# Agent attention and top-1 experts on one core: transfers queued in the order asked for, and longer distances between a chunk's steps

## The chip, the cores and the metric

The kernel runs on one core of a Trainium2 chip. The core has five engines with an instruction stream each: TensorE (PE in the profile; its weight loads are listed as PEld), VectorE (DVE), ScalarE (ACT), GpSimd (POOL) and SyncE (SP), which does nothing here but start transfers and read a few registers. Transfers run on 16 DMA engines. An engine works through its own stream in order and waits at an instruction until what that needs is there. The metric is the device time of one execution in microseconds; the kernel before was timed three times.

## The reference

For each of four batches: agent attention over N = 11456 tokens of 128 numbers with 49 agents, then a mixture of eight experts in which each token goes to one expert.

```python
def sm(a, b):
    s = scale * (a @ b.transpose(0, 2, 1))
    e = np.exp(s - s.max(-1, keepdims=True))
    return e / (e.sum(-1, keepdims=True) + 1e-09)
a2k = sm(agents, k)
agent_v = a2k @ v
x = (sm(q, agents) @ agent_v).reshape(-1, D)
expert_idx = np.argmax(x @ w_gate, axis=1)
...
    xe = x[mask]
    h = np.maximum(xe @ w1[e], 0.0)
    out[mask] = gate_w[mask, None] * (h @ w2[e])
```

All tensors are float32. There are 45824 tokens in all; F, the hidden size of an expert, is 1024.

## The kernel before

**Tiling.** A batch is cut into 12 chunks of tokens: 11 of 1024 (128 partitions, 8 tokens in each) and a remainder of 192. Keys, queries and values of a chunk are loaded into a tile `ld` (512 KB, 11 buffers), squared and summed on ACT for a scale (`squares`, L348), split into two float16 halves `hl` (ACT makes the high half, DVE the low one, L392 and L394), and for keys and queries turned over by a DMA transpose into `hT` (`turn_over`, L415; two buffers for keys, two for queries). PE makes the scores of the chunk from `hT` (L461 to L463). Of queries, ACT takes the exponential E, which is stored to DRAM (`exps`, L699), split into float16 halves in one of two tiles `mm` (L705, L709) and turned over by another DMA transpose into `M` (`eturn`, L712).

**The experts' main loop.** Most tokens of a batch go to one expert, which is worked off for all tokens. `experts` (L1294 to L1346) makes 23 groups of up to 512 tokens times 8 slices of F: 184 steps a batch, 736 in all. One step is two matmuls of 512 columns on PE (L1299, L1300, which read `M`), the high and low float16 halves of their ReLU on ACT (L1305) and on DVE (L1306), and 12 matmuls of 128 columns (L1320), which belong to the step five before. Four PSUM tiles `ph` hold the results of the first two. After eight steps DVE multiplies the group by its gate (L1333) and SP stores it (L1339). Tokens of other experts are gathered in 14 blocks late in the last batch and after it.

**How the work is interleaved.** The attention of batch b + 1 runs beside the experts of batch b. The order is a table of times counted in steps: `at(t, f)` (L275) puts f on a heap, `after(dt, f)` (L279) puts it dt steps behind the event that is running, and the loop at L1396 takes the events in order of time. Step 0 of batch b has time 184 b. Keys of a batch start at `KS`, one chunk every `KT` = 9 steps, and their scores come `KL` steps behind the squares; queries start at `QA`, 8, then 13 steps apart, and their scores also come `KL` behind (`KLL` for the later chunks of the last batch). Values come 5.3 steps apart. `DTR` is the distance from the low half to the transpose into `hT`, `DTE` from the halves of E to the transpose into `M`, `DEX` from the exponential to the store of E, `DST` from the gate's product to the store of a group. A load is asked for when the squares of the second use before it are (`load`, L298: `AHEAD` = 3 uses with the present one).

The keys' exponentials are added up chunk by chunk on POOL into `es` (L555). Then `agentvalues(0)` reduces `es` to `e1` on DVE (L609), and `agentvalues(1)` sums `e1` over the partitions on PE (L614); both are due one and two steps behind the last chunk's exponentials (L891 to L893). POOL also ranks the tokens of the batch that is ending (`leftover_ranks`, L930, L935 to L952) in that time.

**What sets an engine's order.** The framework schedules each engine's stream from the traced program with a model of its own: an instruction that is ready by the model may be taken ahead of others traced earlier. `issue_after` (L1403) ties what an event issues on PE, ACT and DVE behind the step's instruction on the same engine that lies 1.5, 2 and 2.5 steps back. SP has no such tie before the change, apart from a gate at the start (L220): its stream is what the model made of it.

Of the kernel before, what the change touches and what calls it, by code (L numbers as in the profile page):

```python
# [45 lines left out]
KS0, KT0, KL0, VT0, VL0, QS0, QT0, QL0 = -200, 2, 4, 2, 1, -172, 3, 2.5  # L46
VE, T1, TF0, TF1, TL, TLM, Q0 = 12, 1.75, 3, 1.5, 18, 10, 2

KS, KT, VT, VL, VL4, TW0, TW1, DW = -208, 9, 5.3, 8, 5, 8, 2.5, 1
QA, QB, QC, QB3, KL, LL, UD, RG, D1, DL = -20, 8, 13, 10.5, 9, 9.5, 2, 0.7, 0.5, 0  # L50

KS1 = []

KLL, LLL = 11, 11
LX, LMG, LSP = 8, 4, 2.5

SLA, SLD, SLP = 2, 2, 1.5

DTR, DTE, DEX, DST, DXS = 2, 0.5, 2, 2, 0.5

LAG = 5

# [13 lines left out]
def agent_moe_kernel(ctx, tc, q, k, v, agents, wg, w1, w2, out):  # L76
    nc = tc.nc
# [11 lines left out]
    NCK = len(chunks)  # L89
# [177 lines left out]
    def pick(x, c):  # L267
        return x[c % len(x)]
# [4 lines left out]
    now, count = [0], [0]  # L273

    def at(t, f, *a):  # L275
        count[0] += 1
        heapq.heappush(events, (t, count[0], f, a))
# [10 lines left out]
    def attention(b):  # L288
        st = state[b]
        base = b * steps  # L290
        first, last = b == 0, b + 1 == B
# [573 lines left out]
        ks, kt, kl, vt, vl = (KS0, KT0, KL0, VT0, VL0) if first else (KS, KT, KL, VT, VL)  # L865
        dl = 0 if first else DL
# [12 lines left out]
        tv = tk + 4  # L879
# [8 lines left out]
            at(base + t + 2 * dl, kexp3, c)  # L888
            at(base + t + vl, values, c)
        ta = tv + vt * (NCK - 1) + vl + 2  # L890
        te = tv + vt * (NCK - 1) + 2 * dl + (T1 if first else 1)  # L891
        at(base + te, agentvalues, 0)
        at(base + te + (0.1 if first else 1), agentvalues, 1)  # L893
        at(base + ta, agentvalues, 2)
        at(base + ta + 1.5, agentvalues, 3)
        at(base + ta + 2.5, agentvalues, 4)
# [251 lines left out]
    def weights_ahead(u):  # L1148
        T, i, _ = where[u]
        ws[u] = block_weights(T, i, tiles(w1e=(ldp, "ld"), w2e=(ldp, "ld")))  # L1150

    def weights_split(u, j, eng):
        x, (T, i, _) = ws[u][j], where[u]
        m = T["m1" if j == 0 else "m2"][:, i:i + 1]
        tag = slots[(2 * u + j) % len(slots)]
        hl = wsp[u, j] = (ldp if tag == "ld" else xpool).tile(
            [P, 2, FF], F16, tag=tag, name="wsp", **({} if tag == "ld" else dict(bufs=HLB if tag == "hl" else HTB[tag[2:]])))
        nc.scalar.activation(hl[:, 0, :], x, AF.Copy, scale=m)
        if eng == "D":
            nc.vector.scalar_tensor_tensor(hl[:, 1, :], x, m, hl[:, 0, :], op0=ALU.mult, op1=ALU.subtract)  # L1160
        else:
            nc.scalar.activation(x, x, AF.Copy, scale=m)
            nc.gpsimd.tensor_tensor(hl[:, 1, :], x, hl[:, 0, :], op=ALU.subtract)

    def block_layer1(u, hf):

        xs, w = blocks[u][0], wsp[u, 0]
        wv = w.rearrange("d s (p t) -> d s t p", t=FT)
        ph = psH.tile([P, 512], F32, tag="h", name="ph")
        for i in range(4):  # L1170
            o, t = ph[:, i * P:(i + 1) * P], hf * 4 + i
            nc.tensor.matmul(o, wv[:, 0, t, :], xs[:, 0, :], start=True, stop=False)
            nc.tensor.matmul(o, wv[:, 0, t, :], xs[:, 1, :], start=False, stop=False)
            nc.tensor.matmul(o, wv[:, 1, t, :], xs[:, 0, :], start=False, stop=True)
        hh = hpool.tile([P, 2, 512], F16, tag="h", name="hh")
        nc.scalar.activation(hh[:, 0, :], ph, AF.Relu)
        nc.vector.scalar_tensor_tensor(hh[:, 1, :], ph, 0.0, hh[:, 0, :], op0=ALU.max, op1=ALU.subtract)
        bh[u, hf] = hh

    def block_layer2(u, hf):  # L1180

        wv = wsp[u, 1].rearrange("p s (t d) -> p s t d", d=D)
        if hf == 0:
            bh[u] = psY.tile([P, 512], F32, tag="y", name="pyb")
        py, hh = bh[u], bh.pop((u, hf))
        for t in range(hf * 4, hf * 4 + 4):
            x = hh[:, :, t % 4 * P:(t % 4 + 1) * P]
            nc.tensor.matmul(py[:, :D], x[:, 0, :], wv[:, 0, t, :], start=(t == 0), stop=False)
            nc.tensor.matmul(py[:, :D], x[:, 0, :], wv[:, 1, t, :], start=False, stop=False)
            nc.tensor.matmul(py[:, :D], x[:, 1, :], wv[:, 0, t, :], start=False, stop=(t == FT - 1))  # L1190

    def block_store(u):
        _, gt, ti = blocks[u]
        yo = two.tile([P, D], F32, tag="yb", name="yb")
        nc.vector.tensor_scalar(yo, bh.pop(u)[:, :D], gt, None, op0=ALU.mult)
        view = oviews[u]
        rows = B * N
        if where[u][2]:
            rows -= N
            view = view[:rows]  # L1200
        nc.gpsimd.indirect_dma_start(out=view, out_offset=bass.IndirectOffsetOnAxis(ap=ti, axis=0),  # L1201
                                     in_=yo, in_offset=None, bounds_check=rows - 1, oob_is_err=False)
# [167 lines left out]
        for t in dt:  # L1370
            after(t, next, gen, None)

    paced, steps_of = [], []
    for b in range(B):
        attention(b)
        steps_of.append(experts(b))
        turns(steps_of[b], b * steps, 1, steps + LAG + 2)
        turns(leftover_ranks(b), b * steps + (LT3 if b + 1 == B else LT), LTS3 if b + 1 == B else LTS, 6)

    for j in range(2 * E):  # L1380
        b, i = divmod(j, -(-2 * E // (B - 1)))
# [13 lines left out]
    uses = [x[1:] for x in sorted(uses)]  # L1395
    while events:  # L1396
        now[0], _, f, a = heapq.heappop(events)
        with ExitStack() as held:
            if not (f is next and a[0] in steps_of):
                for x, s in ((1, SLP), (2, SLA), (3, SLD)):  # L1400
                    p = next((p for p in reversed(paced) if p[0] <= now[0] - s), None)
                    if p:
                        held.enter_context(tc.issue_after(p[x].ins))  # L1403
            f(*a)
    for u in range(NS + BL):
        for x in range(max(WA, u - BL + SPA), min(NS, u - BL + SPA + 5)):
            if x not in ws:
                weights_ahead(x)
        d = u - BL
        for j in range(2):  # L1410
            if u < NS:
                block_layer1(u, j)
            if d >= 0:
                block_layer2(d, j)
        if d >= 0:
            block_store(d)
            if d + SPA < NS:
                for j in range(2):
                    weights_split(d + SPA, j, pick(TSE, 2 * d + j))
# [57 lines left out]
```

## Time and profile before

| | |
|---|---|
| time, median of three | 1176.09 us (1173.71 to 1177.47) |
| the profiled execution's own time | 1170.0 us |
| span of its instructions | 1168.3 us |
| busy: PE, DVE, ACT, POOL | 1028.7, 1000.3, 830.9, 219.0 us |
| mean granted TensorE clock | 0.962 |
| HBM read and written | 99.75 MB, 36.43 MB |

Terms of the sum are times of the profiled execution. A "wait" of an engine is its idle time just before an instruction, put down to what released it. The DMA share of a stretch is the summed time of its packets over 16 engines; it can pass 1 since packets overlap.

### The profile page before, as it was taken

To read this page: it belongs to the slowest core of one execution; us is meant where nothing else is said; L and a number is where in the kernel's file an instruction comes from. 1 tells how busy PE (TensorE), PEld (TensorE's weight loads), DVE (VectorE), ACT (ScalarE), POOL (GpSimd) and SP (SyncE) were. 2 spreads that over 40 slices of the span, in tenths; PEclk is the share of its full clock that TensorE was granted. 3 is DMA by queue.
4 is the path that set the end of the run, shared out by engine and by line. 5 is a ranking of instruction groups with operands and counts; after the bars stand their busy time and mean duration, and the time that the engine had idled before them with its cause. 6 is when DMAs were issued, how large, how long until landed. Compare 5 with 4: busy or idle time off the path is not lost. (4 is left out here: it accounts for less than half of the span.)

```text
span 1168.3 us, 35751 instructions
## 1 busy us (share of the span) xinstructions
PE 1028.7 (88%) x14575; PEld 826.5 (71%) x14575; DVE 1000.3 (86%) x2372; ACT 830.9 (71%) x1495; POOL 219.0 (19%) x369
## 2 busy tenths in 40 slices
PE   7848998999877999999778999999799899989895
PEld 7826776777666777777666777777577677767794
DVE  5877897998797998998687998999699899899794
ACT  6457776888676877988576877988477566756581
POOL 1300010234200000334200000333200113110133
PEclk9867999999999999999899999999899999999998
DMA  8579978632299988732299889621294554522460
GB/s 316 189 213 256 225 178 208 163 89 68 82 257 285 206 185 202 182 103 83 79 243 288 201 187 199 182 91 65 69 235 103 142 116 106 168 74 84 138 246 14
DMA packets 263592, 190.49 MB, mean 163 GB/s; under 512 B 215433, under 2 KB 228226, under 8 KB 263424
## 3 DMA queue, kind: packets, MB, share of 16 engines
q1 hardware_dynamic: 261856, 185.92, 61.6%
q0 software_dynamic: 1568, 2.25, 0.9%
q8 instruction: 115, 1.88, 0.7%
q14 instruction: 53, 0.43, 0.1%
HBM read 99.75 MB, written 36.43 MB: 117 GB/s over the span
## 5 line engine op out<-in xcount | busy, mean ns | idle before, releaser
L1320 PEld LDWEIGHTS <-hh 128*128 128x128 f16 x8640 | 552.1, 99 | 167.4 <-issue 10.9
L1320 PE MATMUL py<-w2h,hh 128*128 128x128 f16 (+1 forms) x5760 | 611.1, 221 | 0.2 <-DVE mul L233 0.2
L1305 ACT ACTIVATE hh<-ph 128x512 f16<-128x512 f32 (+1 forms) x728 | 408.7, 582 | 199.3 <-PE ph L1300 191.4
L1320 PE MATMUL py<-w2l,hh 128*128 128x128 f16 (+1 forms) x2880 | 527.3, 221 | 0.0
L1306 DVE SCALAR_TENSOR_TENSOR hh<-ph,hh 128x512 f16<-128x512 f32 (+1 forms) x736 | 477.9, 666 | 35.7 <-ACT hh L1305 32.0
L1299 PE MATMUL ph<-M,Ah 128*128 128x512 f16 (+1 forms) x736 | 278.5, 379 | 32.7 <-DVE hh L1306 21.1
L1300 PE MATMUL ph<-M,Al 128*128 128x512 f16 (+1 forms) x736 | 278.8, 379 | 0.2 <-DVE Al L813 0.2
L394 DVE SCALAR_TENSOR_TENSOR hl<-ld,mul,hl 128x1024 f16<-128x1024 f32 (+1 forms) x119 | 144.4, 1219 | 18.1 <-ACT hl L392 17.0
L392 ACT ACTIVATE hl<-ld,mul 128x1024 f16<-128x1024 f32 (+1 forms) x119 | 129.0, 1093 | 22.1 <-DVE mul L233 21.7
L358 ACT ACTIVATE jk<-ld 128x1024 f16<-128x1024 f32 (+1 forms) x126 | 126.2, 1001 | 4.5 <-DMA ld<-in_k_dram 4.4
L236 POOL TENSOR_SCALAR div<-hb,bits 128x1 int32<-128x1 int32 (+1 forms) x90 | 32.2, 358 | 414.0 <-DVE hb L229 397.1
L1300 PEld LDWEIGHTS <-Al 128*128 128x128 f16 x736 | 72.2, 98 | 29.6 <-issue 27.3
L461 PEld LDWEIGHTS <-hT 128*128 128x128 f16 (+1 forms) x622 | 51.9, 98 | 53.2 <-DMA hT<-hl 52.8
L461 PE MATMUL ps_s<-agh,hT 128*128 128x49 f16 x574 | 54.2, 186 | 35.0 <-DMA hT<-hl 33.9
L1299 PEld LDWEIGHTS <-Ah 128*128 128x128 f16 x736 | 73.9, 101 | 11.6 <-DMA M<-mm 7.7
L1333 DVE TENSOR_TENSOR yo<-py,cs 128x512 f32<-128x512 f32 (+1 forms) x92 | 61.5, 668 | 1.4 <-PE py L1320 1.3
L463 PE MATMUL ps_s<-agh,hT 128*128 128x49 f16 x574 | 53.9, 186 | 0.0
L462 PE MATMUL ps_s<-agl,hT 128*128 128x49 f16 x574 | 53.9, 186 | 0.0
L462 PEld LDWEIGHTS <-hT 128*128 128x128 f16 (+1 forms) x622 | 51.5, 99 | 3.4 <-issue 3.2
L555 POOL TENSOR_TENSOR es<-es,S 128x392 f32<-128x392 f32 (+1 forms) x33 | 33.7, 1020 | 103.3 <-ACT S L536 89.4
L463 PEld LDWEIGHTS <-hT 128*128 128x128 f16 (+1 forms) x622 | 51.3, 98 | 0.2
L236 POOL TENSOR_SCALAR div<-hb 128x1 int32<-128x1 int32 (+3 forms) x49 | 12.2, 249 | 180.5 <-DVE hb L229 130.4
(319 smaller groups left out, 1360.3 us busy)
## 6 DMA issues: line engine op xcount, KB each, us to landing
ld<-in_k_dram SPq DMA_DIRECT2D x44, 512.0 KB
ld<-in_v_dram SPq DMA_DIRECT2D x44, 512.0 KB
ld<-in_q_dram SPq DMA_DIRECT2D x44, 512.0 KB
out_dram<-yo SPq DMA_DIRECT2D x88, 256.0 KB
w1e<-in_moe_w_dram SPq DMA_DIRECT2D x18, 512.0 KB
w2e<-in_moe_w_dram SPq DMA_DIRECT2D x18, 512.0 KB
exps<-E SPq DMA_DIRECT2D x44, 196.0 KB
wn<-in_moe_w_dram SPq DMA_DIRECT2D x16, 512.0 KB
```

Of the source, the lines that this page charges most:

```text
L358: nc.scalar.activation(jk[:p, :t * D], x[:p, :t, :].rearrange("p t d -> p (t d)"), AF.Square, accum_out=ss[:p])
L392: nc.scalar.activation(hi[:p, :t, :], x[:p, :t, :], AF.Copy, scale=m)
L394: nc.vector.scalar_tensor_tensor(lo[:p, :t, :], x[:p, :t, :], m, hi[:p, :t, :], op0=ALU.mult, op1=ALU.subtract)
L461: nc.tensor.matmul(o, x[:, 0, i, :p], AG["h"], start=True, stop=False)
L462: nc.tensor.matmul(o, x[:, 0, i, :p], AG["l"], start=False, stop=False)
L463: nc.tensor.matmul(o, x[:, 1, i, :p], AG["h"], start=False, stop=True)
L1299: x1 = nc.tensor.matmul(ph[:, :nn], st['Ah'][:, f, :], m, start=True, stop=False)
L1300: nc.tensor.matmul(ph[:, :nn], st['Al'][:, f, :], m, start=False, stop=True)
L1305: x2 = nc.scalar.activation(hh[:, 0, :nn], ph[:, :nn], AF.Relu)
L1306: x3 = nc.vector.scalar_tensor_tensor(hh[:, 1, :nn], ph[:, :nn], 0.0, hh[:, 0, :nn], op0=ALU.max, op1=ALU.subtract)
L1320: mm_ = lambda l, r, **k: nc.tensor.matmul(o, l, r, skip_group_check=True, **k)
L1333: nc.vector.tensor_tensor(yo[:p, :n, :], py[:p, :n * D].rearrange("p (i d) -> p i d", d=D), cs.unsqueeze(2).broadcast_to([p, n, D]), op=AL ...
```

## The change

Three things are done. The loop that takes the events keeps a list of all instructions that SP was given, and what an event issues on SP is tied behind the last of them, from time 0 on: SP's stream is the order of the events. Distances grow: squares to scores from 9 to 12 steps with the squares three steps earlier (`KS`, `QA`, `KL`; in the first batch the later query chunks keep their start, and their scores come three steps later; in the last batch the later queries' scores come two steps earlier), low half to transpose 2 to 3.5, halves of E to transpose 0.5 to 2, exponential to its store 2 to 3, product to its store 2 to 3. And in batches 1 to 3 the sum over `es` moves from one step behind the last exponentials to five, the sum over partitions from two to six and a half.

```diff
--- before.py
+++ after.py
@@ -46,17 +46,18 @@
 KS0, KT0, KL0, VT0, VL0, QS0, QT0, QL0 = -200, 2, 4, 2, 1, -172, 3, 2.5
 VE, T1, TF0, TF1, TL, TLM, Q0 = 12, 1.75, 3, 1.5, 18, 10, 2
 
-KS, KT, VT, VL, VL4, TW0, TW1, DW = -208, 9, 5.3, 8, 5, 8, 2.5, 1
-QA, QB, QC, QB3, KL, LL, UD, RG, D1, DL = -20, 8, 13, 10.5, 9, 9.5, 2, 0.7, 0.5, 0
+KS, KT, VT, VL, VL4, TW0, TW1, DW = -211, 9, 5.3, 8, 5, 8, 2.5, 1
+QA, QB, QC, QB3, KL, LL, UD, RG, D1, DL = -23, 8, 13, 10.5, 12, 9.5, 2, 0.7, 0.5, 0
 
 KS1 = []
 
-KLL, LLL = 11, 11
+KLL, LLL = 12, 11
 LX, LMG, LSP = 8, 4, 2.5
 
 SLA, SLD, SLP = 2, 2, 1.5
 
-DTR, DTE, DEX, DST, DXS = 2, 0.5, 2, 2, 0.5
+DTR, DTE, DEX, DST, DXS = 3.5, 2, 3, 3, 0.5
+TE0, TE1 = 5, 6.5
 
 LAG = 5
 
@@ -888,9 +889,9 @@
             at(base + t + 2 * dl, kexp3, c)
             at(base + t + vl, values, c)
         ta = tv + vt * (NCK - 1) + vl + 2
-        te = tv + vt * (NCK - 1) + 2 * dl + (T1 if first else 1)
-        at(base + te, agentvalues, 0)
-        at(base + te + (0.1 if first else 1), agentvalues, 1)
+        te = tv + vt * (NCK - 1) + 2 * dl
+        at(base + te + (T1 if first else TE0), agentvalues, 0)
+        at(base + te + (T1 + 0.1 if first else TE1), agentvalues, 1)
         at(base + ta, agentvalues, 2)
         at(base + ta + 1.5, agentvalues, 3)
         at(base + ta + 2.5, agentvalues, 4)
@@ -1370,7 +1371,7 @@
         for t in dt:
             after(t, next, gen, None)
 
-    paced, steps_of = [], []
+    paced, steps_of, queue = [], [], []
     for b in range(B):
         attention(b)
         steps_of.append(experts(b))
@@ -1395,13 +1396,18 @@
     uses = [x[1:] for x in sorted(uses)]
     while events:
         now[0], _, f, a = heapq.heappop(events)
+        traced = nc.cur_bb.bb.instructions
+        seen = len(traced)
         with ExitStack() as held:
+            if now[0] > 0 and queue:
+                held.enter_context(tc.issue_after(queue[-1]))
             if not (f is next and a[0] in steps_of):
                 for x, s in ((1, SLP), (2, SLA), (3, SLD)):
                     p = next((p for p in reversed(paced) if p[0] <= now[0] - s), None)
                     if p:
                         held.enter_context(tc.issue_after(p[x].ins))
             f(*a)
+        queue.extend(i for i in traced[seen:] if i.engine == mybir.EngineType.SP)
     for u in range(NS + BL):
         for x in range(max(WA, u - BL + SPA), min(NS, u - BL + SPA + 5)):
             if x not in ws:
```

SP's stream at the start of batch 2, from behind the experts' weights and ranks to the first transpose into `M` (`ld` is a load, `hT` and `M` are written by transposes), before:

```order
L305 DMA ld<-in_q_dram 128x1024
L420 DMA_TRANSPOSE hT<-hl 128x16x128
L1404 DMA out_dram<-yo 128x512
L305 DMA ld<-in_k_dram 128x1024
L305 DMA ld<-in_q_dram 128x1024
L305 DMA ld<-in_k_dram 128x1024
L420 DMA_TRANSPOSE hT<-hl 128x16x128 x2
L1404 DMA out_dram<-yo 128x512
L305 DMA ld<-in_q_dram 128x1024
L1404 DMA exps<-E 128x392
L305 DMA ld<-in_k_dram 128x1024
L715 DMA_TRANSPOSE M<-mm_143 128x8x128
```

and after:

```order
L961 DMA ranks<-C 128x8x181
L421 DMA_TRANSPOSE hT<-hl 128x16x128
L306 DMA ld<-in_k_dram 128x1024
L1409 DMA out_dram<-yo 128x512
L306 DMA ld<-in_q_dram 128x1024
L421 DMA_TRANSPOSE hT<-hl 128x16x128 x2
L306 DMA ld<-in_k_dram 128x1024
L1409 DMA out_dram<-yo 128x512
L1409 DMA exps<-E 128x392
L306 DMA ld<-in_q_dram 128x1024
L716 DMA_TRANSPOSE M<-mm_143 128x8x128
```

From the first transpose of a key chunk (one row ahead of the first fence, one row ahead of the second) to the transpose into `M` of the batch's first chunk there are three more `hT` transposes in both. Before, six loads stand among them; after, four, with the first `in_q` load moved ahead of the first `hT` and one `in_k` load moved behind `M`; the ranks' store has moved behind the first `hT`.

SP's stream where the first values of batch 2 are loaded, beside batch 1's queries, before:

```order
L305 DMA ld<-in_k_dram 96x256
L305 DMA ld<-in_v_dram 128x1024
L1404 DMA out_dram<-yo 128x512
L420 DMA_TRANSPOSE hT<-hl 128x16x128
L1404 DMA exps<-E 128x392
L305 DMA ld<-in_q_dram 128x1024
L715 DMA_TRANSPOSE M<-mm_143 128x8x128
```

and after:

```order
L306 DMA ld<-in_k_dram 96x256
L1409 DMA out_dram<-yo 128x512
L421 DMA_TRANSPOSE hT<-hl 128x16x128
L306 DMA ld<-in_q_dram 128x1024
L306 DMA ld<-in_v_dram 128x1024
L1409 DMA out_dram<-yo 128x512
L1409 DMA exps<-E 128x392
L716 DMA_TRANSPOSE M<-mm_144 128x8x128
```

The load of values that followed the last key chunk's load at once now stands behind a store, a transpose and a query load; counted from the start of SP's stream it lies twenty transfers later than before.

DVE's stream around the sum over the keys' exponentials of batch 2, before (`S` is the last chunk's scores, `e` the sum over `es`, `hh` one step of the experts each):

```order
L394 SCALAR_TENSOR_TENSOR hl<-ld,mul,hl 96x256
L531 TENSOR_TENSOR S<-S,mxb 96x98
L1306 SCALAR_TENSOR_TENSOR hh<-ph,hh 128x512
L609 TENSOR_REDUCE e_10993<-es 128x49
L1306 SCALAR_TENSOR_TENSOR hh<-ph,hh 128x512
```

and after:

```order
L395 SCALAR_TENSOR_TENSOR hl<-ld,mul,hl 96x256
L532 TENSOR_TENSOR S<-S,mxb 96x98
L1307 SCALAR_TENSOR_TENSOR hh<-ph,hh 128x512 x2
L1334 TENSOR_TENSOR yo<-py,cs 128x512
L1307 SCALAR_TENSOR_TENSOR hh<-ph,hh 128x512 x3
L610 TENSOR_REDUCE e_11104<-es 128x49
```

The reduction that stood one step behind the last subtraction stands five steps behind it.

## Rows read from the trace of the kernel before

**Rows 1.** The page's first two parts: the span, and busy share in 40 equal slices (tenths; PEclk is the granted clock, DMA the mean share of the 16 DMA engines).

```profile
span 1168.3 us, 35751 instructions
PE 1028.7 (88%) x14575; PEld 826.5 (71%) x14575; DVE 1000.3 (86%) x2372; ACT 830.9 (71%) x1495; POOL 219.0 (19%) x369
...
PEclk9867999999999999999899999999899999999998
DMA  8579978632299988732299889621294554522460
```

**Rows 2.** PE's waits over the whole span: the waiting line, what released it, us in total, times, the longest.

```profile
PE ps_s L461 <- DMA hT<-hl: 33.9, 22, 3.7
...
PE ps_small L614 <- DVE e L609: 18.4, 3, 6.8
...
PE ps_y L461 <- DMA hT<-hl: 5.7, 4, 2.8
...
PE ph L1299 <- DMA M<-mm: 3.5, 1, 3.5
```

**Rows 3.** Ten stretches, each a wait of PE for `hT` from its start to 4 us behind its end: us, then busy time of PE, PEld, DVE, ACT, POOL, granted clock, DMA share, GB/s; the last row is the sum of all ten.

```profile
122.40:128.30 5.90, 3.96 (x67) 3.25 (x68) 4.12 (x13) 2.37 (x6) 0.00 (x0) 1.00 1.32 266
...
326.30:332.80 6.50, 3.98 (x67) 3.24 (x67) 4.65 (x23) 4.69 (x10) 0.59 (x2) 1.00 1.08 259
353.10:358.80 5.70, 3.72 (x77) 2.76 (x78) 3.96 (x12) 3.61 (x8) 1.19 (x2) 1.00 1.15 253
374.80:382.30 7.50, 3.95 (x55) 3.17 (x56) 3.94 (x8) 2.02 (x5) 0.00 (x0) 0.80 1.16 251
...
588.20:594.60 6.40, 3.96 (x43) 3.07 (x44) 4.23 (x20) 4.16 (x9) 0.28 (x1) 0.73 1.14 272
638.50:645.70 7.20, 3.93 (x53) 3.38 (x54) 3.56 (x7) 1.56 (x3) 0.00 (x0) 0.76 1.33 278
...
927.10:934.80 7.70, 4.01 (x52) 3.21 (x52) 2.95 (x9) 1.46 (x3) 3.00 (x4) 0.83 0.98 260
sum 65.90, PE 39.44 PEld 31.43 DVE 41.39 ACT 27.27 POOL 5.06; mean PE 3.94 PEld 3.14 DVE 4.14 ACT 2.73 POOL 0.51
```

**Rows 4.** The same view of PE's three waits for the sum over `es`, each to 4 us behind its end.

```profile
295.80:304.70 8.90, 4.03 (x45) 3.17 (x44) 4.56 (x9) 2.39 (x5) 4.20 (x7) 0.81 0.25 88
554.90:565.70 10.80, 4.03 (x42) 3.19 (x42) 4.50 (x9) 3.12 (x7) 7.25 (x23) 0.74 0.22 74
818.40:829.20 10.80, 4.02 (x42) 3.18 (x42) 4.51 (x9) 3.10 (x7) 7.23 (x23) 0.71 0.07 26
sum 30.50, PE 12.08 PEld 9.54 DVE 13.57 ACT 8.61 POOL 18.68; mean PE 4.03 PEld 3.18 DVE 4.52 ACT 2.87 POOL 6.23
```

**Rows 5.** POOL in order of time before the second of these waits ends: start, us, line, operation, in brackets the idle time before it.

```profile
549.87 1.01 POOL L555 TENSOR_TENSOR es<-es,S 128x392 f32<-128x392 f32 x1 [5.50 <-ACT S L536]
550.84 1.78 POOL L935 TENSOR_TENSOR C<-oh,npri 128x720 f32<-128x720 f32 x1
...
560.40 0.39 POOL L555 TENSOR_TENSOR es<-es,S 96x98 f32<-96x98 f32 x1
```

**Rows 6.** DVE in order of time at the same place.

```profile
560.83 0.81 DVE L609 TENSOR_REDUCE e<-es 128x49 f32<-128x392 f32 x1 [6.07 <-POOL es L555]
```

**Rows 7.** The view of rows 3 for PE's two waits for the first `M` of batches 1 and 2, each to 4 us behind its end.

```profile
347.00:354.50 7.50, 2.60 (x27) 1.81 (x26) 4.71 (x11) 3.52 (x9) 0.00 (x0) 1.00 1.13 255
609.70:617.60 7.90, 3.84 (x27) 2.56 (x26) 4.57 (x10) 3.32 (x9) 0.00 (x0) 0.82 1.09 228
```

**Rows 8.** The same view of longer stretches: before, at and behind the start of batches 1 and 2.

```profile
250.00:320.00 70.00, 62.83 (x882) 49.67 (x881) 56.34 (x139) 53.32 (x102) 25.92 (x48) 0.98 0.19 63
320.00:380.00 60.00, 47.58 (x715) 37.50 (x714) 50.47 (x128) 41.87 (x74) 4.14 (x11) 0.99 1.10 272
...
580.00:650.00 70.00, 58.59 (x824) 46.23 (x823) 56.82 (x142) 49.04 (x88) 5.02 (x12) 0.93 1.10 263
```

**Rows 9.** Two stretches with the first matmul of a step alone (L1299): us, then PE busy (times), PEld busy (times), clock, DMA share, GB/s.

```profile
380.00:540.00 160.00, 45.85 (x122) 11.83 (x121) 0.99 0.70 167
650.00:800.00 150.00, 42.74 (x114) 11.03 (x114) 1.00 0.67 163
```

**Rows 10.** The instructions that write `hT`: how long SP is held by one, in ns (least/median/most), first and last start in us.

```profile
L420 SPq DMA_TRANSPOSE hT<-hl x76: 1317/2862/7202, 79.0 to 981.4; - x76
```

**Rows 11.** The same for a load of values, and, of those who waited for `ld`, ACT's squares (us, times).

```profile
L305 SPq DMA_DIRECT2D ld<-in_v_dram x48: 327/544/1291, 10.3 to 753.6; - x48
...
ACT jk L358: 4.4, 2
```

**Rows 12.** SP's own stream in order of time at the start of batch 1: start, us, operation.

```profile
343.11 1.54 SPq L715 DMA_TRANSPOSE M<-mm  x1
...
345.95 8.97 SPq L420 DMA_TRANSPOSE hT<-hl  x2
```

**Rows 13.** The instructions on the second expert weights `w2e`: first and last start. ACT's L827 is the first reader in batch 0, and waited for the load.

```profile
L263 SPq DMA_DIRECT2D w2e<-in_moe_w_dram x18: 332/343/750, 64.4 to 1127.6; - x18
...
L827 ACT ACTIVATE jk<-w2e x4: 1050/1059/1065, 68.9 to 848.8; 128x1024 f16<-128x1024 f32 x4
```

**Rows 14.** The view of rows 3 for the first steps of batch 0, in which PE waits for the first transposes of all.

```profile
82.60:97.60 15.00, 8.48 (x131) 5.91 (x131) 9.61 (x19) 11.14 (x18) 1.67 (x4) 0.50 1.13 207
```

## Prediction, made before the changed kernel was run

> **What bounds the kernel now.** I read the page's busy shares first, then PE's waits, then busy times in short stretches around each long wait. PE is busy for 88% and DVE for 86% of the span [rows 1]; neither is full, and in steady stretches a step takes 1.31 us (160 us for 122 steps, 150 us for 114) [rows 9]. The reader is to see in PE's waits that three kinds stand out: 33.9 + 5.7 us for the transposed keys and queries `hT`, 18.4 us for the sum over the exponentials, 3.5 us for `M` [rows 2] (a second wait for `M`, 609.7 to 613.6, is counted at PE's weight load). All are transfers or helpers that come late; the experts' own chain does not cause them.
>
> A wait of PE costs the kernel only what DVE, the next busiest engine, loses as well. That is why the stretches reach 4 us behind each wait's end: DVE may still be catching up. Ten waits for `hT` fill 65.9 us, of which DVE works 41.39, so it idles 24.5 us [rows 3]; the three for the sum fill 30.5 us, DVE works 13.57 and idles 16.9 [rows 4]; the two for `M` fill 15.4, DVE works 9.28 and idles 6.1 [rows 7]. Together 47.5 us in which both engines stand. Nearly every microsecond of these waits is lost, so taking one away gives it back.
>
> Why are the transfers late? At the start of batches 1 and 2 the DMA engines are full (share 1.10 at 263 to 272 GB/s), while in the 70 us before the first start they are at 0.19 [rows 8]. And SP itself is held: one `hT` transpose occupies it for 2.86 us in the middle, up to 7.2 [rows 10], two in a row for 8.97, where a transpose into `M` just ahead took 1.54 [rows 12].
>
> **The change part by part.** The sums are made against the profiled execution's 1170.0 us (span 1168.3 and 1.7 around it). That is 6.1 us under the median of the runs shown; I take the saving over unchanged.
>
> *Squares to scores, low half to transpose.* The squares and the split come 3 steps earlier, 3.9 us; the transpose is asked for 1.5 steps later behind the split, so 1.5 steps (2.0 us) earlier than before as seen from the scores. No instruction is added. What it is set against: the longest of PE's waits is 3.7 us [rows 2]. Where a wait comes from the split or from SP's being held at the split's result, the full 3.9 us count and it vanishes; where it comes from the queue alone, 2.0 us count. In the second fence of SP's stream two loads of 512 KB fewer lie between the first `hT` and `M`; at 272 GB/s one is 1.9 us. So 3.9 to 5.8 us stand against waits of 2 to 3.7. I take 80% of the 24.5: 19.6 us. Bounds: all of it, 24.5, and nothing, 0, if the full DMA engines only move the wait (a rival below). The first waits of batch 0 (15 us of which DVE idles 5.4) [rows 14] stay, since the transposes there are held back by the gate at L220, which is not touched.
>
> *The sum over `es`.* POOL is in order: the next to last chunk's addition starts at 549.87, then the ranking runs, and the last chunk's addition of 0.39 us comes only at 560.40 [rows 5]; DVE stands 6.07 us for it [rows 6]. Four steps more on DVE and four to five on PE are 5.2 to 5.9 us. POOL's stream keeps the ranking ahead of that addition, so the addition is not earlier. Of the waits of 6.8, 6.8 and 4.9 us about 1.3, 1.3 and 0 remain: 16.9 - 2.6 = 14.3 us gained. Bounds 10 (POOL falls behind further, since PE no longer gives it the pause) and 16.9. What follows, `agentvalues(2)`, is due ten steps behind the exponentials and still finds its sum, 3.5 steps ahead.
>
> *First `M` of a batch.* It is asked for 1.5 steps (2.0 us) later, but the four `hT` transposes and all but one of the loads ahead of it are asked for 3 steps earlier, and a load less lies ahead of it. 6.1 us are to be had; I take half, 3. Bounds 6.1 and, if the 2.0 us decide, -4 for the two batches.
>
> *Stores.* Product to store and exponential to store grow by a step each. By then the value is there, so SP does not stand at a store with transposes behind it. No term of its own; it is what lets the strict order work.
>
> *The strict order itself.* It adds a wait in principle at each of some 500 transfers: whatever comes late on SP holds all behind it. Queued behind are transposes, for which PE waits, and loads, for which ACT's squares wait. Before, loads were taken far ahead, and ACT waited for them 4.4 us in all [rows 11]; that cover goes. A load of values is now asked for as little as 5.3 steps (6.9 us) ahead of its squares. A load that was used at once, the experts' second weights of batch 0, was started at 64.4 and read at 68.9, 4.5 us [rows 13]. 6.9 - 4.5 leaves 2.4 us; a median transpose on SP takes 2.86. So some loads will be late by a fraction of a microsecond, and ACT, busy for 71%, and four `ph` tiles (up to 5.2 us) lie between that and PE. I take 4 us lost in all. Bounds 0 and 48 (the rival below).
>
> Sum: 19.6 + 14.3 + 3 - 4 = 33 us. 1170 - 33 = 1137 for a profiled execution, 1143 for the median of runs. What comes next is DVE: with 1000 us of work in 1135 it is busy for 88%.
>
> A rule of the Trainium skill against the weight I give to SP's order: "DMA: Bandwidth & Descriptors" (Issuing engines are not separate DMA queues) says that the time to initiate a transfer is usually small beside the transfer. The trace disagrees for transposes, with 2.86 us [rows 10] against 0.54 for a load [rows 11]; by the rule, late loads would be no danger, the sum would be 37 and the second rival below would fall away.
>
> **Rivals.**
> 1. *The DMA engines' throughput decides at a batch's start.* The change moves no byte fewer. Then the `hT` waits at 326, 353, 375, 588 and 638 stay (DVE idle 1.85, 1.74, 3.56, 2.17, 3.64 = 13.0) [rows 3] and so do both for `M`. For it: share 1.10 there [rows 8]. Against: loads are now spread, and the start is 3 steps earlier in a time when the engines are nearly empty. Gain: (24.5 - 13.0) x 0.8 + 14.3 - 4 = 19.5; 1157.
> 2. *Slower: late loads of values.* They sit behind transposes that hold SP. Two in a row hold it for 8.97 us [rows 12]; 8.97 + 4.5 - 6.9 = 6.6 us late. If DVE's load leaves only half of the `ph` cover, 2.6, PE stands 4.0 us each time; with four such loads in each of three batches that is 48 us against 37 gained: 11 slower, 1187. It decides from the point where SP is held more than 5 us ahead of such a load (2.4 + 2.6). Against it: in that part of a batch keys are done, and transposes come singly.
> 3. *The clock comes back with the waits.* Around the sum's waits the granted clock is 0.71 to 0.81 [rows 4], and in four of the rows for `hT` 0.73 to 0.83 [rows 3]: part of the time PE runs at 1.2 instead of 2.4 GHz. If PE sets the pace there, (1 - clock) times the stretch is lost, 1.7 + 2.8 + 3.1 and 1.5 + 1.7 + 1.7 + 1.3, together 13.8 us. Gain 33 + 13.8 = 47; 1129, which is also what all 47.5 us without any new wait would give. Against: DVE's idle time in these stretches is not larger than the waits, so DVE paces behind them. The Trainium skill's "TensorE: Matmul & The Clock Gate" (HAM oscillation) counts half of the throttled time as lost, which is this sum.
> 4. *The change does not bite*: the transfers wait for their producers and not for their place, so the order is no different in effect, and the sum's wait moves by as much as its place: 1176.
>
> **How the numbers follow.** The forecast has 0.52 (its own range 1136 to 1151), the first rival 0.20, the second 0.15, the third 0.08, the fourth 0.05. Faster by over 0.3% (3.5 us, about what can be told from no change): 0.52 + 0.20 + 0.08 = 0.80; no change 0.05; slower 0.15. The range from 1116 to 1178 reaches below the third case, since the bounds of the terms do, and over the first and the fourth; it leaves out the slower case and little else.
>
> **What the profile would show.** Right: PE's waits for `hT` at 12 us or less in all, most of it before 100 us; L614 under 4 us in all; in SP's stream no store that stands with a transpose behind it; DVE busy for 88%. The first rival: at the starts of batches 1 and 2 the share stays at 1.1 and the `hT` and `M` waits are still 2 to 4 us. The second: ACT's L358 waits for `ld` in tens of microseconds, and PE for ACT or `ph` between steps 85 and 145. The prediction is wrong if SP, tied to the order of events, runs later than the events ask.

## The result and the profile after

| | before | after |
|---|---|---|
| median (least to most) | 1174.9 us (1170.58 to 1177.47) | 1131.11 us (1129.85 to 1132.92) |
| the profiled execution, its span | 1170.0, 1168.3 us | 1129.85, 1128.1 us |
| granted clock of the profiled execution | 0.962 | 0.969 |

Each median is of four runs. The ratio is 0.9632, 95% interval [0.9599, 0.9665]: 43.8 us faster by the medians, 40.2 by the profiled spans.

The page's first parts, after:

```profile
span 1128.1 us, 35718 instructions
PE 1021.4 (91%) x14575; PEld 823.6 (73%) x14575; DVE 1000.8 (89%) x2372; ACT 829.3 (74%) x1495; POOL 214.5 (19%) x369
...
PEclk9866999999999999999899999999999999999998
DMA  8579789633399998645299998634467653433470
```

Against [rows 1] these lines split the 40.2 us of span. PE stood idle for 1168.3 - 1028.7 = 139.6 us and now for 1128.1 - 1021.4 = 106.7: 32.9 less. And the same 14575 matmuls kept it busy for 7.3 us less: they ran at a higher clock. (By the clock's records in the two traces 62.4 us of PE's busy time lay at the lower level before and 48.7 after; half of the difference is 6.9.) DVE's work is unchanged (1000.3, 1000.8).

PE's waits after, to be held against [rows 2]:

```profile
PE ph L1300 <- DVE hh L1307: 23.6, 36, 1.7
PE ps_s L462 <- DMA hT<-hl: 12.0, 8, 3.0
PE ps_small L325 <- ACT jk L323: 7.2, 2, 3.7
...
PE ps_y L462 <- DMA hT<-hl: 3.3, 2, 2.7
...
PE ps_small L615 <- DVE e L610: 1.6, 1, 1.6
```

The waits for `hT` fell from 39.6 to 15.3 us. The sum over `es` fell from 18.4 to 1.6, but a new wait of 3.7 stands beside it, at the agents' squares (L325): before, that line had one of 3.6. The waits for `M` are counted at PE's weight load:

```profile
PEld L1300 <- DMA M<-mm: 4.9, 2, 2.5
```

The same views of before, with the wait for DVE's half of a step (`hh`):

```profile
PE ph L1299 <- DVE hh L1306: 21.1, 31, 3.9
PE ps_small L324 <- ACT jk L322: 3.6, 1, 3.6
PEld L1299 <- DMA M<-mm: 7.7, 2, 4.0
```

The two waits for `M` before are the first part of the two stretches of [rows 7], 3.5 and 3.9 us on PE; the second is put down to `hh` there, the 3.9 of the first line. Behind all of these the most common wait is now the one for `hh`, 36 short ones.

The new wait stands behind the same late addition. POOL and then DVE at the sum of batch 2, start, us, and in brackets the idle time before:

```profile
532.18 1.02 POOL L556 TENSOR_TENSOR es<-es,S 128x392 f32<-128x392 f32 x1 [5.50 <-ACT S L537]
...
542.72 0.39 POOL L556 TENSOR_TENSOR es<-es,S 96x98 f32<-96x98 f32 x1
```

```profile
543.14 0.81 DVE L610 TENSOR_REDUCE e<-es 128x49 f32<-128x392 f32 x1 [1.98 <-POOL es L556]
...
544.64 0.91 DVE L319 TENSOR_SCALAR ag<-ag 49x128 f32<-49x128 f32 x1
```

From the one addition to the other it is 10.5 us, as in [rows 5]: POOL's ranking is still ahead. DVE's own wait shrank from 6.07 [rows 6] to 1.98, but behind the reduction, in order, DVE has the agents' scaling (L319), which feeds the squares on ACT and PE's L325.

### The profile page after: what moved, and what is told of

Same layout as the page of the kernel before. It is cut to its first block, busy times and chain, and to the rows that moved or that the text cites. A ratio compares the mean times of both kernels' runs of the same rounds, so it can differ in the third digit from the quotient of the medians.

```text
span 1128.1 us, 35718 instructions
## 1 busy us (share of the span) xinstructions
PE 1021.4 (91%) x14575; PEld 823.6 (73%) x14575; DVE 1000.8 (89%) x2372; ACT 829.3 (74%) x1495; POOL 214.5 (19%) x369
## 5 line engine op out<-in xcount | busy, mean ns | idle before, releaser
L1300 PE MATMUL ph<-M,Ah 128*128 128x512 f16 (+1 forms) x736 | 276.7, 376 | 35.3 <-DVE hh L1307 23.6
L395 DVE SCALAR_TENSOR_TENSOR hl<-ld,mul,hl 128x1024 f16<-128x1024 f32 (+1 forms) x119 | 148.5, 1255 | 14.6 <-ACT hl L393 12.0
L237 POOL TENSOR_SCALAR div<-hb,bits 128x1 int32<-128x1 int32 (+1 forms) x90 | 27.0, 300 | 470.3 <-DVE hb L230 443.9
L462 PEld LDWEIGHTS <-hT 128*128 128x128 f16 (+1 forms) x622 | 52.7, 99 | 23.5 <-DMA hT<-hl 22.8
L462 PE MATMUL ps_s<-agh,hT 128*128 128x49 f16 x558 | 52.6, 186 | 13.8 <-DMA hT<-hl 12.0
L464 PE MATMUL ps_s<-agh,hT 128*128 128x49 f16 x558 | 52.3, 186 | 0.0
L699 ACT ACTIVATE E<-E,ln,div 128x392 f32<-128x392 f32 (+1 forms) x47 | 32.4, 689 | 14.1 <-DVE E L693 13.2
```

The source lines that it names most:

```text
L395: nc.vector.scalar_tensor_tensor(lo[:p, :t, :], x[:p, :t, :], m, hi[:p, :t, :], op0=ALU.mult, op1=ALU.subtract)
L462: nc.tensor.matmul(o, x[:, 0, i, :p], AG["h"], start=True, stop=False)
L464: nc.tensor.matmul(o, x[:, 1, i, :p], AG["h"], start=False, stop=True)
L1300: x1 = nc.tensor.matmul(ph[:, :nn], st['Ah'][:, f, :], m, start=True, stop=False)
```

## The experiments

All ratios are to the kernel before, run on the same chip; after is at 0.9632 by this measure. "Waits" are PE's in the profiled execution; for `hT` the two lines (L461 or L462) are added.

**1. The order alone.** The kernel before with the list and the tie, its distances and its sum unchanged.

```diff
+            if now[0] > 0 and queue:
+                held.enter_context(tc.issue_after(queue[-1]))
...
+        queue.extend(i for i in traced[seen:] if i.engine == mybir.EngineType.SP)
```

> The kernel before with SP's transfers tied to the order of the events, no distance changed. Theory A (the distances give the time back, the order only lets them): the transposes are asked for as late as before, SP now also stands at stores two steps behind their product, so no gain and perhaps a loss: -5 to +10 us against before; PE's waits for hT stay above 30 us, the sum's wait stays at 17 to 19. Theory B (loads taken ahead of the transposes were the harm, and the order alone removes it): 15 to 25 us faster, waits for hT under 20 us.

Measured: 1170.33 us, ratio 0.9984 [0.9954, 1.0014]. Two of its waits:

```profile
PE ps_s L461 <- DMA hT<-hl: 36.8, 21, 3.4
PE ps_small L614 <- DVE e L609: 18.9, 4, 6.8
```

The order by itself is worth nothing, and it harms nothing that shows in the time: the waits are much those of [rows 2] (`hT` 36.8 + 6.9 us, 4.1 more than before). At PE's weight load the waits for `M` fell from 7.7 to 1.6 us. On SP the order removes a hold of its own: before, SP stood 63.6 us in front of the loads of expert weights (L1018) whose buffer was still being read; here that is gone, and SP stands longer at stores instead (148.7 us at those for DVE's products, where it was 130.6).

**2. The distances alone.** The changed kernel without the tie and with the sum back at one and two steps.

```diff
-TE0, TE1 = 5, 6.5
+TE0, TE1 = 1, 2
...
-            if now[0] > 0 and queue:
-                held.enter_context(tc.issue_after(queue[-1]))
```

> The changed kernel without the tie on SP and with the sum over the exponentials back at one and two steps: only the longer distances. Theory A: the hT waits fall to 15 to 20 us, 15 to 22 us faster than before, the sum's wait unchanged at 17 to 19. Theory B: the loads still stand ahead of the transposes and the hT waits stay near 30 us: 0 to 8 us faster.

Measured: 1151.9 us, ratio 0.9815 [0.9784, 0.9847]: some 22 us by the ratio, 20 by the medians. Waits for `hT` 13.6 + 4.4 us, for the sum 18.0 as before, for `M` 8.4 at the weight load.

**3. The sum alone.** The kernel before with `agentvalues(0)` and `(1)` five and six and a half steps behind the exponentials.

> The kernel before with only the sum over the exponentials moved (five and six and a half steps). Both theories: 11 to 16 us faster than before, PE's waits at the sum (and at the agents' squares behind it) fall from 18.4 to 3 to 7 us, the hT waits stay at 35 to 42. If it gains under 7 us, the pause at the sum had been filled with work that now stands elsewhere.

Measured: 1149.35 us, ratio 0.9786 [0.9755, 0.9818]: some 25 us by the ratio, 22 by the medians, where 11 to 16 were expected.

```profile
PE ps_small L615 <- DVE e L610: 3.8, 3, 1.7
```

The wait at the sum is 3.8 us where it was 18.4, of PE's other long waits none moved by more than 4, and still more came back than the whole wait: a first sign that a wait may cost more than its own length. The profiled execution alone doesn't show it: its span is 17.1 us shorter.

**4. All but the order.** The changed kernel without the tie.

> The changed kernel without the tie on SP. Theory A: 28 to 36 us faster than before, so the order itself is worth 6 to 14 of the 43. Theory B: 12 to 20 us faster, and the order is worth the rest. If it is as fast as the changed kernel, the order is worth nothing.

Measured: 1137.59 us, ratio 0.97 [0.9653, 0.9748]. The order adds 0.7% to it, some 8 us by the ratios and 6.5 by the medians; the intervals overlap slightly. The gains of runs 2 and 3 (0.0185 + 0.0214 = 0.040) are more than the 0.030 that both give together.

**5. The scores back.** The changed kernel with the old distance from squares to scores; the order, the requests and the sum as changed.

```diff
-KS, KT, VT, VL, VL4, TW0, TW1, DW = -211, 9, 5.3, 8, 5, 8, 2.5, 1
-QA, QB, QC, QB3, KL, LL, UD, RG, D1, DL = -23, 8, 13, 10.5, 12, 9.5, 2, 0.7, 0.5, 0
+KS, KT, VT, VL, VL4, TW0, TW1, DW = -208, 9, 5.3, 8, 5, 8, 2.5, 1
+QA, QB, QC, QB3, KL, LL, UD, RG, D1, DL = -20, 8, 13, 10.5, 9, 9.5, 2, 0.7, 0.5, 0
...
-KLL, LLL = 12, 11
+KLL, LLL = 11, 11
```

> The changed kernel with the squares and the scores back at nine steps (eleven for the last batch's later queries), all else as changed. Theory A (the lead of the transposes over the scores gives the waits back): 15 to 22 us slower than the changed kernel, so about 0.980 against before, hT waits 30 us or more, since the transposes are now asked for 1.5 steps later than in the kernel before. Theory B (order and sum give all): within 5 us of the changed kernel.

Measured: 1159.62 us, ratio 0.986 [0.9842, 0.9878]: 27 us slower than after by the ratios, 28 by the medians, more than either theory said. Its longest group of waits:

```profile
PE ps_s L462 <- DMA hT<-hl: 39.4, 28, 3.5
```

With 2.8 us at the other line it is 42.2, 2.6 more than before and 27 more than in after: this one distance carries the gain at `hT`. The run is also slower than run 3, which has the sum alone. A transpose asked for 1.5 steps later, with nothing earlier ahead of it, was expected to come later, but the waits for `hT` are only 1.7 us longer than in run 3 (40.5), so the cause of the rest isn't shown.

**6. The requests back.** The changed kernel with the four old distances to transposes and stores.

```diff
-DTR, DTE, DEX, DST, DXS = 3.5, 2, 3, 3, 0.5
+DTR, DTE, DEX, DST, DXS = 2, 0.5, 2, 2, 0.5
```

> The changed kernel with the distances to the transposes and stores back at 2, 0.5, 2 and 2 steps; SP's order stays tied. Theory A: SP stands at stores and transposes whose values are not yet there and holds the others behind: 5 to 12 us slower than the changed kernel (0.968 to 0.974 against before). Rival: the transposes are asked for 1.5 steps earlier and SP never stands for long: the same or up to 4 us faster.

Measured: 1130.77 us, ratio 0.9615 [0.9597, 0.9632], as after. Waits for `hT` were lower (8.1 + 2.9 us), `M` gave none, and in their place stood two for `Al` (L814), a product with the experts' weights that DVE splits into halves:

```profile
PE ps_small L844 <- DVE Al L814: 7.9, 2, 4.2
```

So with the strict order these four distances bring nothing on balance. ACT's squares waited for loads for 21.2 us here, 15.0 of them for queries, and the time is that of after: if late loads on ACT cost the kernel anything here, it is no more than the other waits gave back.

**7. Loads earlier.** The changed kernel with `AHEAD` 6 instead of 3, so that loads are asked for three uses sooner.

> The changed kernel with loads asked for five uses ahead instead of two. If late loads cost it anything (my term of 4 us), this gives up to 4 us back. If loads ahead of the transposes were the harm that the order took away, hT waits rise and it is 3 to 10 us slower. If neither, the same within 3 us.

Measured: 1130.25 us, ratio 0.9604 [0.9572, 0.9635], as after. Neither theory of harm holds: the loads of the changed kernel were not late enough to cost anything, and three loads more ahead of nearly every transpose from batch 1 on, which is what the edit makes of SP's stream, did not delay them (waits for `hT` 15.1 us, 15.3 in after). ACT's wait for keys' loads in the changed kernel itself, to be held against [rows 11]:

```profile
ACT jk L359 <- DMA ld<-in_k_dram: 3.9, 1, 3.9
ACT jk L359 <- DMA ld<-in_q_dram: 1.0, 2, 0.6
```

4.9 us in all where it was 4.4, and no line for a load of values.

**8. Still longer.** The changed kernel with three more steps from squares to scores and two more to the sum.

```diff
-KS, KT, VT, VL, VL4, TW0, TW1, DW = -211, 9, 5.3, 8, 5, 8, 2.5, 1
-QA, QB, QC, QB3, KL, LL, UD, RG, D1, DL = -23, 8, 13, 10.5, 12, 9.5, 2, 0.7, 0.5, 0
+KS, KT, VT, VL, VL4, TW0, TW1, DW = -214, 9, 5.3, 8, 5, 8, 2.5, 1
+QA, QB, QC, QB3, KL, LL, UD, RG, D1, DL = -26, 8, 13, 10.5, 15, 9.5, 2, 0.7, 0.5, 0
...
-KLL, LLL = 12, 11
+KLL, LLL = 15, 11
...
-TE0, TE1 = 5, 6.5
+TE0, TE1 = 7, 8.5
```

> The changed kernel with the squares another three steps ahead of the scores (15 steps) and the sum another two steps later (seven, eight and a half). Theory A: the remaining waits are 15 us for hT, of which 8.6 lie in the first steps and stay, 4.6 for M and 5.3 at the sum; 8 to 12 us of these go, 1119 to 1123. Rival (the DMA engines' throughput at a batch's start sets what is left there): only the sum's 5 us go, 1125 to 1128.

Measured: 1118.33 us, ratio 0.9501 [0.9484, 0.9518]: the fastest of all, 13 us under after. Waits for `hT` 6.9 us, clock 0.976:

```profile
PE ps_y L462 <- DMA hT<-hl: 3.7, 2, 3.1
PE ps_s L462 <- DMA hT<-hl: 3.2, 2, 1.8
```

**9. PE kept at work in the wait.** The kernel before with matmuls that nobody reads ahead of the sum.

```diff
+                for i in range(0 if first else 80):
+                    nc.tensor.matmul(pt[:, :P], ones16, ones16, start=True, stop=True)
```

> The kernel before, with 80 matmuls of 128 columns put on PE right ahead of the sum over es in batches 1 to 3; nobody reads what they write. In the trace of the kernel before, 128-column matmuls start 55 ns apart, so 80 take 4.4 us, inside waits of 4.9, 6.8 and 6.8 us. The waits themselves stay. Theory of the clock: behind the wait at 555 to 561 us the clock of before is 0.50 for 4 us and 0.75 for 4 more, and in the second of these DVE works only 1.7 of 4 us, so PE paces there; with PE at work in the wait the clock stays at 1.0 behind it and each wait costs 2 to 3 us less: 1164 to 1170 where before is 1174, ratio 0.992 to 0.996, and the granted clock in the 8 us behind each wait is over 0.9. Rival theory, the forecast's: DVE, behind by the length of the wait, paces there and the clock costs nothing: ratio 1.000 within 0.002, whatever the clock. If the matmuls run at the lower clock they outlast the wait: 2 to 4 us slower each, ratio above 1.004.

Measured: 1171.6 us, ratio 0.9976 [0.9949, 1.0004]; as a whole not told apart from no change. The stretches behind the waits tell more. In the kernel before, two of 4 us each behind PE's second wait for the sum: us, busy time of PE, PEld, DVE, ACT, POOL, granted clock, DMA share, GB/s.

```profile
561.70:565.70 4.00, 4.00 (x41) 3.18 (x42) 3.62 (x8) 0.60 (x1) 1.64 (x3) 0.50 0.19 70
565.70:569.70 4.00, 4.00 (x44) 3.11 (x43) 1.61 (x4) 1.95 (x4) 0.00 (x0) 0.84 0.00 0
```

The same two in the run with the matmuls:

```profile
564.10:568.10 4.00, 3.95 (x64) 3.24 (x65) 3.97 (x9) 1.44 (x3) 1.70 (x3) 1.00 0.17 66
568.10:572.10 4.00, 4.00 (x57) 3.17 (x55) 2.69 (x7) 3.14 (x7) 0.00 (x0) 1.00 0.00 0
```

PE made 121 matmuls in the 8 us instead of 85. The matmuls themselves and the sum behind them:

```profile
557.21 4.63 PE L614 MATMUL ps_small<-ones 128*128 128x128 bf16 x80
564.15 0.42 PE L616 MATMUL ps_small<-e,ones 128*128 128x49 f32 x2 [2.31 <-DVE e L609]
```

From the start of the sum to the start of a step some 16 to 19 us later, the thirteenth in both traces, it took 18.62 us before and 16.17 with the matmuls; the distance from the last step ahead of the wait to the sum is the same (8.03, 8.04). So 2.4 us were lost behind this wait, beside its own 6.8. Most of it is lost at once: the second step behind the sum starts 3.62 us after it before and 1.97 with the matmuls. At the first wait it is 1.55 us, at the third, where the clock fell to 0.66 all the same, 0.6. Run 1, whose waits at the sum are as long and which has no such matmuls, tells how much of this two traces can differ by themselves: the same three distances are 17.67, 18.48 and 17.44 us there, 17.74, 18.62 and 18.02 before and 16.18, 16.17 and 17.45 here. So the first two differences, 4.0 us together, are the matmuls', and the third is not told apart. That is inside the interval of the whole (6.0 gained to 0.5 lost), whose middle lies between the ranges of the two theories.

**10. The sum later, alone.** The changed kernel with `TE0`, `TE1` at 7 and 8.5.

> The changed kernel with the sum over es two steps later still (7 and 8.5 behind the exponentials instead of 5 and 6.5). Left of that wait in the changed kernel are 1.6 us at the sum and 7.2 us at the agents' squares, of which 3.7 us go back to the same late addition. If the 13 us that the still longer distances gained come from this sum: 1120 to 1125. If they come from the distance of squares to scores: 1127 to 1131, at most 4 us gained, since 5.3 us at the sum and the squares are all there is.

Measured: 1123.62 us, ratio 0.9566 [0.9513, 0.962]. The middle value says that some 7 of run 8's 13 us come from the sum; the interval touches those of after and of run 8, so the share isn't settled. The waits at the sum and at the agents' squares, together, fell by 3.3 us.

**11. Still longer without the order.** Run 8 without the tie.

> The still longer distances without the strict order. If the order is worth its 8 us whatever the distances, since it puts the transposes ahead of the later loads: about 1126, with more waits for hT. If the order only makes up for distances that are too short: within 3 us of 1118.

Measured: 1156.27 us, ratio 0.9845 [0.9781, 0.991]: 38 us slower than run 8, and slower than run 4. Its waits for `M`:

```profile
PE ps_s L725 <- DMA M<-mm: 14.6, 3, 5.9
PE ph L1300 <- DMA M<-mm: 10.0, 3, 4.0
```

SP's own stream ahead of the last of these (a wait of 3.96 us for the first `M` of the last batch, which ended at 852.52), start, us, operation:

```profile
841.62 0.33 SPq L1409 DMA_DIRECT2D exps<-E  x1
841.99 0.43 SPq L306 DMA_DIRECT2D ld<-in_q_dram  x1
842.53 5.33 SPq L421 DMA_TRANSPOSE hT<-hl  x1
847.96 1.25 SPq L716 DMA_TRANSPOSE M<-mm  x1
```

The same place in run 8, where PE did not wait for this `M`:

```profile
817.25 0.33 SPq L1409 DMA_DIRECT2D exps<-E  x1
818.78 1.24 SPq L716 DMA_TRANSPOSE M<-mm  x1
820.11 2.34 SPq L421 DMA_TRANSPOSE hT<-hl  x1
```

In the order of the events `M` goes ahead of this `hT`; the framework's model had put it behind, and four loads ahead of it as well. Counted over the whole stream, run 11 has up to nine loads more ahead of an `M` than run 8, an `hT` more ahead of three of the 48, and one fewer ahead of two. Which of the two makes the other waits isn't settled: at the start of batch 1 `M` has its place among the `hT` in both runs, with one load more ahead of it in run 11, and PE waits 3.7 us for it there and 2.2 in run 8. That the model has more to choose from the longer the distances are fits these runs and is not shown by them.

**12. Longer again.** Run 8 with four more steps from squares to scores.

> Four steps more from squares to scores than in the still longer version (KS -218, QA -30, KL 19, KLL 19, Q0 -2), the sum as there. Waits for hT were 6.8 us there, nearly all of them in the first batch behind the gate, which the distances don't move; M is left with 5.3 us. If the distances are used up: within 3 us of 1118. If the starts of the batches still gain by an earlier request: 1110 to 1114. If squares and transposes so early push into the previous batch's end and hold ACT or SP there: 1122 or more.

One constant was left where run 8 has it, against the text above: `KLL` is 15, so the later queries' scores of the last batch come four steps earlier and not at their old place.

Measured: 1135.33 us, ratio 0.967 [0.9617, 0.9724], 17 us over run 8: in the range of the third theory. Its sign came too, by way of DVE and POOL:

```profile
DVE bits L331 <- POOL div L237: 13.3, 2, 7.1
SPq L1409 <- DVE agl L342: 33.0, 2, 16.6
PE ph L1300 <- DVE hh L1307: 31.4, 39, 4.3
```

Before one of the first kind DVE stood 7.1 us, until 293.32, for an operation of 0.21 us on POOL, which lay behind the ranking there. It belongs to the agents' squares of the next batch, four steps earlier than in run 8. Behind DVE's wait PE stood 4.35 us for `hh`, until 294.12, and SP, which had started nothing since 278.4, gave out the next store at 294.87. In run 8 the line of `bits` has 6.7 us in two waits, and PE's for `hh` is

```profile
PE ph L1300 <- DVE hh L1307: 16.8, 30, 1.7
```

so 14.6 us of the difference stand at `hh`, the largest part of it. At PE's weight load `M` rose from 5.6 to 8.3 us as well. What each of these took from the 17 us, and what the change at the last batch's queries did, isn't settled.

## Why the prediction was right, and where its size was off

1131.11 lies within the range, 12 us under the predicted 1143; the direction and the two main causes held. Of the forecast's 33 us the profiled executions gave 40.2.

**The waits, 33 forecast, 32.9 of PE's idle time gone.** That the numbers agree owes something to errors that cancel:

- *Squares to scores*, 19.6: PE's waits for `hT` fell by 24.3 (39.6 to 15.3), at the upper bound. Runs 2 and 5 show that the distance does it: without the order and the sum 18.0 us are left, and without the distance 42.2. The reason given, 3.9 to 5.8 us of lead against waits of 2 to 3.7, held for most of them. Of the 15.3 us left, 9.1 lie in the first steps of batch 0 (75 to 110 us), as said; 12 in all had been forecast. The other 6.2, in waits of up to 3.0, went with three steps more (run 8).
- *The sum*, 14.3: 18.4 fell to 1.6, less the 3.7 that came up at L325, so 13.1. The mechanism held (POOL's chain of 10.5 us is unchanged), but the forecast put the remainder at L614; it did not name the agents' scaling that stands behind the reduction on DVE.
- *First `M`*, 3: two waits of 3.5 and 3.9 became 4.9 in all, 2.5 gained. The order alone brings them to 1.6 (run 1), the distances alone leave them at 8.4 (run 2). So it was the order that moved them. Whether it did so by the loads or by the transposes that it takes from ahead of an `M` isn't shown; with three loads back ahead of it, 6.4 us stand at the weight load (run 7).
- *Late loads*, -4: nothing. ACT waited for loads 4.9 us instead of 4.4, none of them of values, and run 7 gained nothing from loads asked for three uses earlier. This is the step that failed outright, "some loads will be late by a fraction of a microsecond", and the step from there to PE is doubtful too: in run 6 ACT did wait for loads for 21.2 us, and the time stayed that of after. The first reader of `w2e` [rows 13] was taken as the price of a load of values; that load ran at 300 GB/s of traffic (64.4 to 68.9 us), where 163 GB/s flow while the values of batch 2 are loaded in the changed kernel (430 to 510 us). That this is why 4.5 us was too much is likely and not shown.
- *Stores*, nothing: the reason given was wrong, the result right. SP still stands 101.1 us at stores for DVE's products (L1409), where 130.6 were spent before. With the two old distances it stands 134.6 us there, and the time is the same (run 6).
- Not forecast: the waits for `hh` grew. Of the 21.1 us before, 3.9 are the second wait for `M`; from the 17.2 that are left to 23.6 it is 6.4 more, and with that the terms add up: 24.3 + 13.1 + 2.5 - 6.4 = 33.5. That DVE came closer to the bound (busy for 89%, where 88 were said) would fit, but run 8 has 16.8 us of such waits at the same share, so the cause stays open.

**The clock, nothing forecast, at most some 7 us.** The step that failed is the argument against the third rival: "DVE's idle time in these stretches is not larger than the waits, so DVE paces behind them". The stretches of [rows 3, 4] end 4 us behind each wait. Up to there DVE looks like the one that paces: it worked 3.62 of 4 us (run 9's first fence). But PE was full in the same 4 us, at a clock of 0.50; the 4.03 us of PE in each of [rows 4] are these. With the matmuls PE went through its steps there faster, and 1.65 of the 2.4 us are gained in them: DVE was busy, but PE paced. In the next 4 us DVE worked 1.61 with PE at 4.00 and a clock of 0.84, which is beyond the stretches that were read. Run 9 shows at two of the three waits for the sum that this is a cost and not a companion: with PE kept at work the clock stayed at 1.00, and 1.5 and 2.4 us came back. For the whole kernel its interval still holds no change. For run 3, with more gained than the wait was long, the clock is a possible reason and no more: its four executions have a mean clock of 0.9665, the thirteen of before on the same chip 0.9562, but in its trace PE's busy time is 1028.0 us against 1028.7. The rival itself put 13.8 us on the clock; the profiled executions give 7.3 (PE's busy time), and a part of that may lie where DVE paces. The rest of the difference between 40.2 and 43.8 is that the profiled execution before was one of the quicker ones.

In the changed kernel the same can be read behind the wait that is left, in two stretches:

```profile
543.00:547.00 4.00, 0.90 (x5) 0.90 (x6) 3.46 (x7) 1.35 (x4) 2.56 (x7) 0.80 0.32 128
547.00:551.00 4.00, 4.00 (x24) 2.60 (x25) 2.31 (x11) 2.60 (x6) 0.50 (x2) 0.50 0.00 0
```

PE is full at 0.50, the lower of its two levels (1.2 GHz), and DVE works 2.31 of 4. The Trainium skill ("TensorE: Matmul & The Clock Gate", HAM oscillation) counts half of the throttled time as lost. By the two stretches before run 9's matmuls, (1 - 0.50) x 4 + (1 - 0.84) x 4 = 2.64 us were lost at that wait; run 9 got 2.4 of it back, so here the trace agrees with the rule.

**The first rival**, throughput at the starts of batches, may explain what is left. Two stretches over the starts of batches 1 and 2, after:

```profile
310.00:370.00 60.00, 54.90 (x802) 43.88 (x800) 53.48 (x139) 47.40 (x83) 4.38 (x13) 0.94 1.01 240
560.00:630.00 70.00, 62.66 (x891) 49.95 (x890) 61.91 (x157) 53.88 (x94) 4.94 (x14) 0.95 1.00 225
```

The share is still 1.0, as against 1.10 in [rows 8], and `M` is still waited for there; no run tests whether throughput is the reason. But of the `hT` waits one of 1.9 and one of 3.0 us are left in these two stretches, and in the 70 us ahead of batch 1 the share rose from 0.19 [rows 8] to 0.34: a part of the transfers moved into time that was nearly empty. What speaks for full engines does not by itself say that an earlier request is useless. **The second rival**, late loads, fell with run 7. **The fourth**, that the change does not bite, holds for two parts of it: the order alone (run 1) and the four request distances beside all else (run 6) are worth nothing. But the order cannot be struck from the change: it is worth 0 with the old distances, some 8 us with the changed ones, where the intervals overlap, and 38 with longer ones (runs 1, 4, 11). The forecast booked the order as a loss of 4 us, to be made up by the distances. The runs show that the order is what lets the distances grow.

## What to carry to other kernels

Look at PE itself behind a wait of PE, for as long as the clock is low: where it is full at the lower clock, the wait can cost its length and then the clock's share on top, however busy another engine looks beside it. Lengthen distances and fix the issuing queue's order together: the order looked worthless alone and was worth the more the longer the distances were. Try the next longer distance too, since the best of those tried lay one step beyond this change and another step was too far. Where a short helper stands in order behind a long piece of work on the same engine, moving its reader takes the wait away only as far as the next reader allows: of 18.4 us, 3.7 came up again there.

## What was not expected of the hardware

A wait of 6.8 us was followed by 4 us at a clock of 0.50 and 4 more at 0.84, though the clock read 0.93 in the six microseconds of the wait itself: the price falls behind the wait. And 80 matmuls, started 56 ns apart (4.63 us in all), inside the wait kept it at 1.00 behind it in two of three places.

Over 17 runs of the kernel before, the time goes with the clock at 0.60 us for each microsecond of (1 - clock) x span, correlation 0.83, with clocks from 0.949 to 0.964: some two thirds of the spread between its executions. This is an association over runs and not an experiment.
